# Two token tiles per state burst and two token chunks per denominator burst, in a gated mix of linear attention and dilated local attention

## Chip, cores and metric

The kernel runs on one core of a Trainium2 chip. The metric is device time in microseconds, the median of several executions. Nearly all differences in this study are below 0.3% (1.5 us of 488), so each run was timed in rounds with the kernel before on the same chip. A ratio is the mean time of one kernel's fast runs over the mean of the other's in the same rounds; it is not quite the ratio of the quoted medians.

## The reference

Two attention blocks read the same tokens (2048 tokens, width 1024, 32 heads of 32) and are mixed by a gate per token.

```python
g = sigmoid((x * gate_w).sum(-1))
a = A(x, A_wqkv, A_wo)      # linear attention
b = B(x, B_wqkv, B_wo)      # softmax over 8 keys, 2 tokens apart
return g * a + (1 - g) * b
# A: phi(t) = where(t > 0, t + 1, exp(t)) + 1e-6
#    kv  = sum over tokens of phi(k) outer v     (a 32x32 state per head)
#    z   = sum over tokens of phi(k)
#    o   = phi(q) @ kv / (phi(q) . z + 1e-6);  A = o @ wo
```

The *state* of A is `kv` with `z` as a 33rd column. The *denominator* is `phi(q) . z`.

## The kernel before

The program makes a list of operations, each with an engine, an assumed cost, operands and a priority. A list scheduler orders them per engine, and the order is then fixed: every engine executes its list, waiting on semaphores. PSUM banks are chosen while the list is made. The kernel plans six times and keeps the plan whose estimated length is least.

```python
class Pool:                                   # who gets which PSUM bank
    def next(self):
        if seen is None:                      # first plan: in turn
            b = self.bs[self.n % len(self.bs)]
        else:                                 # later plans: the bank that the plan before freed first
            b = min((b for b in self.bs if ...), key=lambda b: seen[b.take] ...)
        ...

for _ in range(PASSES):                       # PASSES = 6
    got = plan(seen)
    seen = got[2]
    if best is None or got[0].span < best[0].span:
        best = got
```

The stages on TensorE are: B's values; B's keys and queries; A's keys and values (16 token tiles of 128); A's query features (4 token chunks of 512, 8 groups each); A's outputs; B's final product. Between dense groups (8 matmuls of 128x128 by 128x512) there are bursts of small matmuls:

* *scores* and *values* of B's local attention, 18 times each;
* *state*, one burst per token tile, into a PSUM bank, which VectorE adds to a running sum:

```python
def state(t, pkt, azt):
    bank = main.next()
    def fn(e):
        for s in range(8):
            for c in range(4):
                h = 16 * (s // 4) + 4 * c + s % 4
                last = e.matmul(bank.ap()[32*c:32*c+32, s*33:s*33+33], pkt[:, h*32:(h+1)*32], azt[:, h, :],
                                start=True, stop=True, tile_position=(0, 32 * c))
        return last
    P.op("pe", fn, 0.22, mode="c", ...)
    # VectorE: copy (t == 0), otherwise kva += bank
...
states.append((slot_n[0] + 4, lambda ...: state(t, pkt, azt)))     # some groups after its tile
```

* *folds*: the state is multiplied into A's output weights (4 bursts); a fold needs four banks at once;
* *denominators*, one burst per chunk of 512 tokens. ScalarE makes reciprocals, DMAs write them to memory and read them back broadcast over 32 rows, and VectorE multiplies the query features by them:

```python
def over(u):                                   # chunk u
    db = main.next()
    # 8 matmuls of 128x32 by 128x512, four column tiles at a time
    P.op("pe", fn, 0.55, mode="c", ...)
    # ScalarE: Ln, Exp(-x);  4 writes to memory
    for j in range(8):                         # read back, multiply
        P.op("sp", ... dma_start(B, src), ..., lat=1.0)
        P.op("dve", ... tensor_tensor(dst, dst, B, ALU.mult), 0.65, ...)

for n, (u, j) in enumerate(nums):              # 32 query groups
    numer(u, j)
    if j == 7:
        after(3, lambda u=u: over(u))
    ...
    if n >= 20:
        a_out(*outs.pop(0))                    # an output may not start before its chunk is divided
EARLY = 3
for t in range(EARLY):                         # some of B's final tiles go between outputs
    while len(outs) > 8:
        a_out(*outs.pop(0))
    final(t)
while outs:
    a_out(*outs.pop(0))
```

## Time and profile before

| | before |
|---|---|
| time, median of the first 3 runs | 488.56 us |
| span of the profiled run | 486.2 us |
| TensorE busy | 474.9 us |
| VectorE busy | 288.4 us |
| dense matmuls, start to start | 215.8 ns |

The page of the kernel before: engines (busy us, share of the span, instructions), and the chain of work that ended last.

```profile
span 486.2 us, 10107 instructions
...
PE 474.9 (98%) x4336; PEld 222.2 (46%) x4403; DVE 288.4 (59%) x557; ACT 139.0 (29%) x225; POOL 5.5 (1%) x34
...
PE 95%; DVE 2%; issue 1%; DMA 1%; SPq 0%; ACT 0%; DVEq 0%
```

TensorE is the limit everywhere, so only what shortens TensorE's own list, or one of its few waits, counts.

What TensorE waited for in the kernel before (us in total, times, longest):

```profile
PE ps_all L1333 <- issue: 3.2, 20, 0.2
PE ps_all L1372 <- DVE warm L1282: 1.3, 1, 1.3
PE ps_all L1333 <- DMA xT<-in_A_x_dram: 0.8, 2, 0.6
PE ps_all L1333 <- DVE rs L1471: 0.5, 3, 0.2
PE ps_all L1333 <- ACT e L1340: 0.2, 1, 0.2
```

The timeline of TensorE in the kernel before (start us, duration us, line, instruction, out<-in, form, count, idle before): one state burst by itself, one behind a values burst, then the four denominator bursts.

```profile
201.85 0.38 PE L1547 MATMUL ps_all<-az,pk 128*32 128x33 bf16 x32
202.17 3.63 PE L1333 MATMUL ps_all<-w,xT 128*128 128x512 bf16 x15
205.73 0.68 PE L1462 MATMUL ps_all<-v,E 64*57 64x33 bf16 x64
206.34 0.38 PE L1547 MATMUL ps_all<-az,pk 128*32 128x33 bf16 x32
...
331.96 0.61 PE L1626 MATMUL ps_all<-pq,zsel 128*32 128x512 bf16 x8
...
348.15 0.62 PE L1626 MATMUL ps_all<-xT,zsel 128*32 128x512 bf16 x8
...
366.07 0.61 PE L1626 MATMUL ps_all<-xT,zsel 128*32 128x512 bf16 x8
...
394.35 0.62 PE L1626 MATMUL ps_all<-xT,zsel 128*32 128x512 bf16 x8
```

A duration in these rows is not what a burst costs, since neighbouring rows overlap (the dense row starts at 202.17 us, before the state row ends at 202.23). The cost is read from the dense matmuls on its two sides: from the start of the last dense one before it to the start of the first one after it, less the 215.8 ns that the first of them takes anyway. A state burst alone comes to 0.405 us, a denominator burst to 0.641 us.

### The profile page before, as it was taken

How to read it: one execution, taken by the hardware profiler on the slowest of the kernel's cores; microseconds unless marked ns; L12 is line 12 of the kernel's file. 1: busy time of each engine (PE TensorE's matmuls, PEld its weight loads, DVE VectorE, ACT ScalarE, POOL GpSimd, SP SyncE). 2: the span in 40 equal slices, each digit the busy share in tenths (PEclk: the TensorE clock that was granted, in tenths of full speed). 3: DMA queues.
4: the chain of work that ended last, by engine and by line, in shares of the span. 5: the costliest groups of instructions: out<-in, count | busy, mean ns of one | idle time of the engine just before them, and what ended most of it. 6: DMA issues, size and time to landing. Idle time of an engine off the chain costs nothing.

```text
span 486.2 us, 10107 instructions
## 1 busy us (share of the span) xinstructions
PE 474.9 (98%) x4336; PEld 222.2 (46%) x4403; DVE 288.4 (59%) x557; ACT 139.0 (29%) x225; POOL 5.5 (1%) x34
## 2 busy tenths in 40 slices
PE   8999999999999999999999999999999999999997
PEld 3444444444444444444444544444444444444443
DVE  2112336899788888575666656596865735434444
ACT  2111111214322233324534333455423322010000
POOL 4000000000000000000000000000000000000000
PEclk9999999999999999999999999999999999999999
DMA  8999992222014459423312322822674316101212
GB/s 221 225 208 309 357 361 63 85 89 87 2 43 142 106 153 233 99 77 84 77 44 65 98 55 48 200 51 41 160 190 98 99 17 179 43 24 44 88 67 89
DMA packets 72951, 57.39 MB, mean 118 GB/s; under 512 B 37953, under 2 KB 60865, under 8 KB 72898
## 3 DMA queue, kind: packets, MB, share of 16 engines
q1 hardware_dynamic: 72210, 56.07, 43.1%
q8 instruction: 36, 0.59, 0.5%
q10 hardware_dynamic: 688, 0.59, 0.4%
q14 instruction: 17, 0.14, 0.1%
HBM read 34.49 MB, written 13.76 MB: 99 GB/s over the span
## 4 chain that ended last, share of the span: by engine, by line
PE 95%; DVE 2%; issue 1%; DMA 1%; SPq 0%; ACT 0%; DVEq 0%
PE ps_all L1333 78%; PE ps_all L1675 11%; PE ps_all L1462 2%; PE ps_all L1439 2%; DMA xT<-in_A_x_dram 1%; PE ps_all L1547 1%; DVE zsel L1589 1%; PE ps_all L1626 0%; DVE pq L1346 0%; SPq L1307 0%; PE ps_all L1599 0%; SPq L1312 0%; DVE rs L1471 0%; DVE e L1344 0%; ACT e L1340 0%
## 5 line engine op out<-in xcount | busy, mean ns | idle before, releaser
L1333 PE MATMUL ps_all<-w,xT 128*128 128x512 bf16 x921 | 209.1, 379 | 4.6 <-issue 1.9
L1333 PE MATMUL ps_all<-xT,w 128*128 128x512 bf16 x747 | 168.3, 379 | 2.0 <-issue 1.3
L1333 PEld LDWEIGHTS ps_all<-w,xT 128*128 128x128 bf16 x960 | 91.1, 98 | 109.6 <-DMA xT<-in_A_x_dram 1.8
L1333 PEld LDWEIGHTS ps_all<-xT,w 128*128 128x128 bf16 x768 | 73.7, 98 | 89.0 <-issue 1.8
L1675 PE MATMUL ps_all<-w,qT 128*128 128x512 bf16 (+1 forms) x259 | 55.3, 372 | 0.3
L1675 PEld LDWEIGHTS ps_all<-w,qT 128*128 128x128 bf16 x264 | 25.8, 98 | 29.7
L1364 DVE CAST vst<-ps_all 128x512 bf16<-128x512 f32 x15 | 10.4, 694 | 43.1 <-PE ps_all L1333 43.1
L1447 ACT ACTIVATE E<-ps_all 128x1824 bf16<-128x1824 f32 (+1 forms) x18 | 30.4, 1687 | 13.4 <-PE ps_all L1439 13.4
L1344 DVE TENSOR_SCALAR e<-e 128x512 bf16<-128x512 bf16 x64 | 17.9, 283 | 26.6 <-ACT e L1342 15.6
L1679 DVE SCALAR_TENSOR_TENSOR o<-ps_all,gm,xT 128x512 bf16<-128x512 f32 (+1 forms) x25 | 18.1, 729 | 23.1 <-PE ps_all L1675 22.9
L1342 ACT ACTIVATE e<-ps_all 128x512 bf16<-128x512 f32 x32 | 19.1, 597 | 42.8 <-PE ps_all L1333 42.8
L1340 ACT ACTIVATE e<-ps_all 128x512 bf16<-128x512 f32 x32 | 19.1, 597 | 36.1 <-PE ps_all L1333 35.3
L1294 DVE TENSOR_TENSOR mx<-mx,kT 128x1024 bf16<-128x1024 bf16 x32 | 20.7, 686 | 9.3 <-ACT kT L1365 9.2
L1294 DVE TENSOR_TENSOR mx<-mx,qT 128x1024 bf16<-128x1024 bf16 x32 | 20.8, 686 | 6.6 <-ACT qT L1368 6.6
L1365 ACT ACTIVATE az<-ps_all 128x512 bf16<-128x512 f32 x22 | 13.2, 599 | 38.3 <-PE ps_all L1333 38.3
L1365 ACT ACTIVATE vst<-ps_all 128x512 bf16<-128x512 f32 x17 | 10.2, 599 | 47.5 <-PE ps_all L1333 47.5
L1473 DVE TENSOR_TENSOR ot<-ps_all,rs 128x512 bf16<-128x512 f32 x36 | 23.6, 683 | 0.2 <-DVE rs L1471 0.2
L1450 DVE TENSOR_TENSOR E<-E,msk 128x1824 bf16<-128x1824 bf16 (+1 forms) x18 | 19.9, 1103 | 5.8 <-ACT E L1447 5.2
L1346 DVE SCALAR_TENSOR_TENSOR pk<-ps_all,e 128x512 bf16<-128x512 f32 x32 | 21.9, 687 | 0.6
L1365 ACT ACTIVATE kT<-ps_all 128x512 bf16<-128x512 f32 x17 | 10.1, 597 | 39.8 <-PE ps_all L1333 39.8
L1368 ACT ACTIVATE qT<-ps_all 128x512 bf16<-128x512 f32 x17 | 10.1, 597 | 39.0 <-PE ps_all L1333 38.9
L1642 DVE TENSOR_TENSOR xT<-xT,rb 128x512 bf16<-128x512 bf16 x24 | 16.3, 688 | 8.5 <-DMA rb<-rc_hbm 8.4
(72 smaller groups left out, 259.1 us busy)
## 6 DMA issues: line engine op xcount, KB each, us to landing
rb<-rc_hbm SPq DMA_DIRECT2D x32, 256.0 KB, 5.0
w<-in_A_wqkv_dram SPq DMA_DIRECT2D x6, 1024.0 KB, 8.6
v<-vB_hbm SPq DMA_DIRECT2D x36, 132.0 KB, 3.0
vB_hbm<-vst SPq DMA_DIRECT2D x32, 132.0 KB, 6.2
w<-in_B_wqkv_dram SPq DMA_DIRECT2D x4, 1024.0 KB, 8.6
xn<-in_A_x_dram SPq DMA_DIRECT2D x16, 256.0 KB, 2.8
out_dram<-o SPq DMA_DIRECT2D x15, 256.0 KB, 2.1
oB_hbm<-ot SPq DMA_DIRECT2D x36, 96.0 KB, 2.1
```

Source lines behind the costliest of these rows:

```text
L1294: P.op("dve", lambda e, m=m, op=op: e.tensor_tensor(m[:, 0:n], m[:, 0:n], src, op), 0.08 + n / 1920.0, reads=[m.all(), reg], writes=[m.all()],
L1333: last = e.matmul(bank.ap(), lhs(dc), rhs(dc), start=(dc == 0), stop=(dc == 7))
L1340: P.op("act", lambda e: e.activation(e_[:, :], bank.ap(), ACT.Exp), act(512), reads=[bank.iv], writes=[e_.all()])
L1342: P.op("act", lambda e: e.activation(e_[:, :], bank.ap(), ACT.Exp, accum_out=qe[:, col:col + 1]), act(512) + 0.1, reads=[bank.iv], writes= ...
L1344: P.op("dve", lambda e: e.tensor_scalar(e_[:, :], e_[:, :], 1.0, 1e-6, op0=ALU.min, op1=ALU.add), 0.25, reads=[e_.all()], writes=[e_.all()])
L1346: P.op("dve", lambda e: e.scalar_tensor_tensor(out=dst, in0=bank.ap(), scalar=0.0, in1=e_[:, :], op0=ALU.max, op1=ALU.add), dps(512), read ...
L1365: fa = lambda e: e.activation(dst, src(), ACT.Copy)
L1447: P.op("act", lambda e: e.activation(E[:, 0:32 * nq].rearrange("p (j q) -> p j q", j=4), ps[:, 4:8, 0:8 * nq], ACT.Exp), act(32 * nq), rea ...
L1450: P.op("dve", lambda e: e.tensor_tensor(ev(), ev(), m[:, :, :].rearrange("p r q -> p (r q)")[:, None, :].to_broadcast([128, 16, 2 * nq]), ...
L1473: P.op("dve", lambda e, r=r, bv=bv, h=h: e.tensor_tensor(o[:, 512 * h:512 * h + 512].rearrange("p (k i c) -> p k i c", k=2, c=32), bv()[:, ...
L1675: last = e.matmul(bank.ap(0, f1 - f0), qT[:, dc, t * 128:(t + 1) * 128], ws[3][:, dc, f0:f1], start=(dc == 0), stop=(dc == 7))
L1679: P.op("dve", lambda e, bank=bank, o_=o_, t=t, n=n, i0=i0, i1=i1, tgt=tgt, c0=c0: e.scalar_tensor_tensor(out=o_[:, i0 * 128:i1 * 128].rear ...
```

## The change

State bursts take two token tiles, accumulate them in PSUM, and ride inside a values burst, so that TensorE's tiling mode changes less often; VectorE adds half as often. Denominator bursts take two chunks. Since the first chunk's reciprocals come later for that, the scheduler gets a later landing time for the broadcast reads, the multiplications get a lower priority, five instead of three of B's final tiles go between the outputs, and they go ahead of the last 16 outputs instead of the last 8. Buffers for two more token tiles are found by moving other buffers.

```diff
@@ landing model: how long after its queue turn a DMA is taken to have landed
-                fin = dma_free + 2.0
+                fin = dma_free + o.pad                  # 2.0 unless given
@@ buffers
-    vr = Ring([... "v%d" ... range(3)])
+    vr = Ring([... "v%d" ... range(2)])
-    pk = Ring([... range(2)]);  az = Ring([... range(2)])
+    pk = Ring([... range(4)]);  az = Ring([... range(4)])
@@ values burst
-                P.op("pe", each, 0.55, mode="c", ..., name="PV")
+                fns, rd, wr, add = [each], [vt.all(), E.all()], [s.iv for s in SO], None
+                if len(states) > 1 and states[1][0] <= slot_n[0]:
+                    fn, more, bank, add = state([states.pop(0)[1] for _ in range(2)])
+                    fns, rd, wr = fns + [fn], rd + more, wr + [bank.iv]
+                P.op("pe", lambda e: [f(e) for f in fns][-1], ...)
@@ a pair that found no values burst
+            if len(states) > 1 and states[1][0] + 2 <= slot_n[0] and not later:
+                ...                                     # a burst of its own
@@ state of two tiles
                 for s in range(8):
-                    for c in range(4):
-                        ... start=True, stop=True, tile_position=(0, 32 * c))
+                    for i, (t, pkt, azt) in enumerate(two):
+                        for c in range(4):
+                            ... start=(i == 0), stop=(i == len(two) - 1), tile_position=(0, 32 * c))
@@ denominators of two chunks
-        def over(u):
-            db = main.next()
+        def over(*us):
+            dbs = [main.next() for _ in us]
             ...                                         # one burst, then Ln, Exp, writes, reads per chunk
-                                  chan="rci%d" % bs, lat=1.0)
+                                  chan="rci%d" % bs, lat=0.6, pad=4.0)
-                P.op("dve", ... ALU.mult), 0.65, ...)
+                P.op("dve", ... ALU.mult), 0.65, ..., prio=1000 + len(P.ops) + (120 if u % 2 else 80))
-            if j == 7:
-                after(3, lambda u=u: over(u))
+            if j == 7 and u % 2:
+                after(3, lambda u=u: over(u - 1, u))
-        EARLY = 3
+        EARLY = 5
-            while len(outs) > 8:
+            while len(outs) > 16:
```

More of the change, by code (lines that the diff above doesn't have):

```diff
@@ L59 @@
 class Op:
-    __slots__ = ("eng", "fn", "cost", "deps", "prio", "seq", "chan", "lat", "pos", "val", "users", "raw", "name", "mode", "start", "end")
+    __slots__ = ("eng", "fn", "cost", "deps", "prio", "seq", "chan", "lat", "pos", "val", "users", "raw", "name", "mode", "pad", "start", "end")
 class Prog:
@@ L78, in __init__, with op @@
         self.read = set()
-    def op(self, eng, fn, cost, reads=(), writes=(), prio=None, chan=None, lat=0.0, after=(), name="", mode="m"):
+    def op(self, eng, fn, cost, reads=(), writes=(), prio=None, chan=None, lat=0.0, after=(), name="", mode="m", pad=2.0):
         o = Op()
+        o.pad = pad
         o.eng, o.fn, o.cost, o.prio, o.chan, o.lat, o.name, o.mode = eng, fn, cost, prio, chan, lat, name, mode
@@ L1186, in build_kernel @@
     eps = SB([128, 1], F32, "eps")
-    gwb = SB([128, 1024], BF16, "gwb")
     gt = SB([128, NT], F32, "gt")
@@ L1196, in build_kernel @@
     flag = SB([1, 1], I32, "flag")
-    warm = SB([128, 512], BF16, "warm")
     er = Ring([SB([128, 512], BF16, "e%d" % i) for i in range(3)])
@@ L1206, in build_kernel @@
     rs = Ring([SB([128, 16], F32, "rs%d" % i) for i in range(4)])
-    vr = Ring([SB([128, 33 * H], BF16, "v%d" % i) for i in range(3)])
-    mtmp = [SB([128, 2, 57], BF16, "mt%d" % i, at=vr.t[2].lo + 256 * i) for i in range(2)]
+    vr = Ring([SB([128, 33 * H], BF16, "v%d" % i) for i in range(2)])
+    mtmp = [SB([128, 2, 57], BF16, "mt%d" % i, at=ot.t[1].lo + 256 * i) for i in range(2)]
     base[0] = max(base[0], top_)
@@ L1212, in build_kernel @@
     RBr = Ring([SB([128, 512], F32, "rb%d" % i, at=kT.lo + 2048 * i) for i in range(12)])
-    mxr = SB([1, 4, 128], F32, "mxr", at=vr.t[2].lo)
+    mxr = SB([1, 4, 128], F32, "mxr", at=ot.t[1].lo)
     ph = base[0]
     mx = [SB([128, 1024], BF16, "mx%d" % i, at=ph + 2048 * i) for i in range(2)]
-    pk = Ring([SB([128, 1024], BF16, "pk%d" % i) for i in range(2)])
-    az = Ring([SB([128, H, 33], BF16, "az%d" % i) for i in range(2)])
+    pk = Ring([SB([128, 1024], BF16, "pk%d" % i) for i in range(4)])
+    az = Ring([SB([128, H, 33], BF16, "az%d" % i) for i in range(4)])
+    warm = SB([128, 512], BF16, "warm", at=pk.t[2].lo)
+    gwb = SB([128, 1024], BF16, "gwb", at=pk.t[3].lo)
     xn = Ring([SB([128, 1024], BF16, "xn%d" % i, at=az.t[i].lo) for i in range(2)])
@@ L1464, in each @@
                     return last
-                P.op("pe", each, 0.55, mode="c", reads=[vt.all(), E.all()], writes=[s.iv for s in SO], name="PV")
+                fns, rd, wr, add = [each], [vt.all(), E.all()], [s.iv for s in SO], None
+                if len(states) > 1 and states[1][0] <= slot_n[0]:
+                    fn, more, bank, add = state([states.pop(0)[1] for _ in range(2)])
+                    fns, rd, wr = fns + [fn], rd + more, wr + [bank.iv]
+                P.op("pe", lambda e: [f(e) for f in fns][-1], 0.55 + 0.5 * (len(fns) - 1), mode="c", reads=rd, writes=wr, name="PV" if add is None else "PV+kv")
+                if add is not None:
+                    add()
                 o, os_ = ot.next()
@@ L1496, in slot @@
                 later.pop(0)[1]()
-            while states and states[0][0] <= slot_n[0]:
-                states.pop(0)[1]()
+            if len(states) > 1 and states[1][0] + 2 <= slot_n[0] and not later:
+                fn, rd, bank, add = state([states.pop(0)[1] for _ in range(2)])
+                P.op("pe", fn, 0.42, mode="c", reads=rd, writes=[bank.iv], name="kv")
+                add()
             pace[0] = min(pace[0] + rate, 1.0) if todo else 0.0
@@ L1537, in plan, with state, add @@
             P.op("pool", lambda e, z=z: e.memset(z[:, :, 32:33], 1.0), 0.2, writes=[z.part((0, H), (32, 33))])
-        def state(t, pkt, azt):
+        def state(two):
             bank = main.next()
             def fn(e):
-                last = None
                 for s in range(8):
-                    for c in range(4):
-                        h = 16 * (s // 4) + 4 * c + s % 4
-                        last = e.matmul(bank.ap()[32 * c:32 * c + 32, s * 33:s * 33 + 33], pkt[:, h * 32:(h + 1) * 32], azt[:, h, :],
-                                        start=True, stop=True, tile_position=(0, 32 * c))
-                return last
-            P.op("pe", fn, 0.22, mode="c", reads=[pkt.all(), azt.all()], writes=[bank.iv], name="kv")
-            src = lambda: bank.ap(0, 264).rearrange("p (i c) -> p i c", c=33)
-            if t == 0:
-                P.op("dve", lambda e: e.tensor_copy(kva[:, :, :], src()), dps(264), reads=[bank.iv], writes=[kva.all()])
-            else:
-                P.op("dve", lambda e: e.tensor_tensor(kva[:, :, :], src(), kva[:, :, :], ALU.add), dps(264), reads=[bank.iv, kva.all()], writes=[kva.all()])
+                    for i, (t, pkt, azt) in enumerate(two):
+                        for c in range(4):
+                            h = 16 * (s // 4) + 4 * c + s % 4
+                            last = e.matmul(bank.ap()[32 * c:32 * c + 32, s * 33:s * 33 + 33], pkt[:, h * 32:(h + 1) * 32], azt[:, h, :],
+                                            start=(i == 0), stop=(i == len(two) - 1), tile_position=(0, 32 * c))
+                return last
+            def add():
+                src = lambda: bank.ap(0, 264).rearrange("p (i c) -> p i c", c=33)
+                if two[0][0] == 0:
+                    P.op("dve", lambda e: e.tensor_copy(kva[:, :, :], src()), dps(264), reads=[bank.iv], writes=[kva.all()])
+                else:
+                    P.op("dve", lambda e: e.tensor_tensor(kva[:, :, :], src(), kva[:, :, :], ALU.add), dps(264), reads=[bank.iv, kva.all()], writes=[kva.all()])
+            return fn, [x.all() for _, p, a in two for x in (p, a)], bank, add
         for t in range(NT):
@@ L1573, in plan @@
                 if r == 3:
-                    states.append((slot_n[0] + 4, lambda t=t, pkt=pkt, azt=azt: state(t, pkt, azt)))
+                    states.append((slot_n[0] + 1, (t, pkt, azt)))
                 slot(FILL)
@@ L1617, in plan, with fn, spread @@
         last_in = [None]
-        def over(u):
-            tgt, c0 = pqn(u)
-            db = main.next()
-            def fn(e):
-                for q in range(2):
-                    for c in range(4):
-                        last = e.matmul(db.ap()[32 * c:32 * c + 32, :], zsel[:, 2 * c + q, :], tgt[:, 2 * c + q, c0:c0 + 512], start=(q == 0), stop=(q == 1),
-                                        tile_position=(0, 32 * c), skip_group_check=True)
-                return last
-            P.op("pe", fn, 0.55, mode="c", reads=[zsel.all(), tgt.part((0, 8), (c0, c0 + 512))], writes=[db.iv], name="den")
+        def over(*us):
+            dbs = [main.next() for _ in us]
+            def fn(e):
+                for u, db in zip(us, dbs):
+                    tgt, c0 = pqn(u)
+                    for q in range(2):
+                        for c in range(4):
+                            last = e.matmul(db.ap()[32 * c:32 * c + 32, :], zsel[:, 2 * c + q, :], tgt[:, 2 * c + q, c0:c0 + 512], start=(q == 0), stop=(q == 1),
+                                            tile_position=(0, 32 * c), skip_group_check=True)
+                return last
+            P.op("pe", fn, 0.1 + 0.45 * len(us), mode="c", reads=[zsel.all()] + [t.part((0, 8), (c, c + 512)) for t, c in map(pqn, us)], writes=[db.iv for db in dbs], name="den")
+            for u, db in zip(us, dbs):
+                spread(u, db)
+        def spread(u, db):
+            tgt, c0 = pqn(u)
             R, rs = RAr.next()
@@ L1639, in over @@
                 last_in[0] = P.op("sp", lambda e, B=B, src=src: e.dma_start(B[:, :], src), 0.5, reads=[[("R", 4 * u + j // 2, 4 * u + j // 2 + 1, None)]], writes=[B.all()],
-                                  chan="rci%d" % bs, lat=1.0)
+                                  chan="rci%d" % bs, lat=0.6, pad=4.0)
                 dst, reg = tgt[:, j, c0:c0 + 512], tgt.part((j, j + 1), (c0, c0 + 512))
-                P.op("dve", lambda e, B=B, dst=dst: e.tensor_tensor(dst, dst, B[:, :], ALU.mult), 0.65, reads=[reg, B.all()], writes=[reg])
+                P.op("dve", lambda e, B=B, dst=dst: e.tensor_tensor(dst, dst, B[:, :], ALU.mult), 0.65, reads=[reg, B.all()], writes=[reg],
+                     prio=1000 + len(P.ops) + (120 if u % 2 else 80))
         def a_loc(t):
```

## The prediction

> **What bounds the kernel.** TensorE. The page gives PE 98% busy of a 486.2 us span, the chain of waits is 95% PE, and PE's wait list holds 6 us in all. In the timeline the dense 128x512 matmuls start 215.8 ns apart everywhere; 2048 of them (by the code) are 442 us. The other 44 us are the start (first dense work at 7 us), the tail, and bursts of small matmuls. From the starts of the dense matmuls around each burst, less 215.8 ns, a burst costs: scores 0.63 us (18 times), values 0.94 (18), state alone 0.405 (5 of 16), state beside values 0.307 more (11 of 16), denominators 0.64 (4). DVE (59%), ACT (29%) and DMA are no limits.
>
> **Taken off TensorE.** The matmuls stay; only drains go. The Trainium skill, "TensorEngine Tiling (Array Packing)", Key Properties, says a change of tiling mode drains the array. The trace agrees: state costs 0.405 us between dense groups and 0.307 where it shares the switch with values, so a saved switch is worth 0.10 us. By the code's slot arithmetic 7 of 8 pairs ride in a values burst and the last stands alone: 7 x 0.614 + 0.71 = 5.0 us against 5.4, a gain of 0.4. Denominators: 0.64 us is two rounds of 0.216 and 0.21 of drain; two bursts of four rounds save 2 x 0.21 = 0.4. Together 0.8 us, all on the critical path.
>
> **Elsewhere.** Eight of 16 state additions on DVE go (0.40 us each): not critical, worth nothing.
>
> **Given back.** The first chunk's denominators move from 332 us to about 345.5. From a denominator burst to the eighth multiplication took 17.2 to 18 us in all four (1.5 us of ACT, 3.2 of write issues, reads at about 1 us each). With the longer burst, and some of the second chunk's writes going first, chunk 0 is ready at about 363 to 366 us (estimate from these). The A outputs, which now start at 352, must wait for it; TensorE can run the query groups of chunks 2 and 3 meanwhile, but each waiting output already owns one of 8 PSUM banks, in program order. After nine query groups (about 362 us) the banks run out: a possible hole of 0 to 4 us at 360 to 368 us. A hole over 1 us has one chance in two. For chunks 2 and 3 the five early final tiles (17 us) and four outputs (7 us) cover the delay. The values' readout starts up to 0.6 us later, as the fused burst signals once; 3.4 us of dense work hides it.
>
> **Predicted time.** 488.3 us: 0.8 us of drains gone, part given back. Without a hole 487.7. Range 487.1 to 490.8. Faster by over 2%: 0.01; within 2%: 0.97; slower by over 2%: 0.02.
>
> **What would show it.** State bursts of 64 matmuls directly behind values (1.55 us extra together), two denominator bursts of 1.07 us, state additions x8, dense pace unchanged. The hole: PE idle before an output group, released by DVE's multiplication by the reciprocals, between 355 and 370 us; without it PE's waits stay near 6 us.
>
> **What would make it wrong.** Accumulating twice into the same 33 columns back to back could run slower than 9.6 ns a matmul; late reads could block DVE, in its fixed order, ahead of evacuations and hold TensorE for several us in the last stage; the new static order could disturb scores and values in the middle.

## The result

| | before | after |
|---|---|---|
| median, 6 runs each | 488.48 us | 487.43 us |
| lowest to highest | 488.10 to 489.16 | 487.20 to 487.88 |
| ratio, 95% interval | | 0.9979 (0.9967 to 0.9992) |
| span of the profiled run | 486.2 us | 486.0 us |
| TensorE busy / VectorE busy | 474.9 / 288.4 us | 474.7 / 285.2 us |
| state | 16 bursts, 5 of them alone | 8 bursts, 1 of them alone |
| denominators | 4 bursts of 0.641 us | 2 bursts of 1.073 us |

The change gains 1.05 us. The page of the changed kernel:

```profile
span 486.0 us, 10106 instructions
...
PE 474.7 (98%) x4339; PEld 223.0 (46%) x4403; DVE 285.2 (59%) x547; ACT 140.2 (29%) x227; POOL 5.9 (1%) x36
...
PE 95%; DVE 2%; issue 1%; DMA 1%; SPq 0%; ACT 0%
```

What TensorE waited for in the changed kernel:

```profile
PE ps_all L1334 <- issue: 3.5, 22, 0.2
PE ps_all L1373 <- DVE warm L1283: 1.3, 1, 1.3
PE ps_all L1334 <- DMA xT<-in_A_x_dram: 0.6, 2, 0.4
PE ps_all L1610 <- DVE pq L1347: 0.5, 1, 0.5
PE ps_all L1334 <- DMA w<-in_B_wqkv_dram: 0.2, 1, 0.2
PE ps_all L1334 <- ACT e L1341: 0.2, 1, 0.2
```

The fourth row is new: a weight fold (line 1610) waits 0.5 us for an evacuation of query features on VectorE. There is no wait for a multiplication by the reciprocals.

The timeline of TensorE in the changed kernel: a values burst with a state pair, the waiting fold, and the stage of the denominators.

```profile
197.12 0.68 PE L1463 MATMUL ps_all<-v,E 64*57 64x33 bf16 x64
197.74 0.66 PE L1556 MATMUL ps_all<-az,pk 128*32 128x33 bf16 x64
...
322.22 0.44 PE L1610 MATMUL ps_all<-w,kvT 32*32 32x512 bf16 x16 [0.50 <-DVE pq L1347]
...
346.08 0.61 PE L1638 MATMUL ps_all<-pq,zsel 128*32 128x512 bf16 x8
346.52 0.60 PE L1638 MATMUL ps_all<-xT,zsel 128*32 128x512 bf16 x8
347.06 22.62 PE L1334 MATMUL ps_all<-xT,w 128*128 128x512 bf16 x102
369.52 13.98 PE L1334 MATMUL ps_all<-w,pq 128*128 128x512 bf16 x62
...
393.79 1.05 PE L1638 MATMUL ps_all<-xT,zsel 128*32 128x512 bf16 x16
```

Behind the first denominator pair all 13 remaining query groups run without a gap, 347.1 to 369.5 us, and only then the outputs of chunk 0 (`w,pq`). The hole that I feared between 360 and 368 us did not open.

One caution about the two traces. The start-up, up to the arrival of the first tokens and weights, is luck: the first scores matmul started anywhere from 128.77 to 129.95 us in the 14 traces of this study. A spread of 1.2 us is more than the effect. So I compare traces by the time from the start of the first scores matmul to the end of the last matmul. It is 354.00 us before and 353.37 us after: 0.63 us less, where the medians say 1.05. The difference of 0.4 us was the first open question.

### The profile page after: what moved, and what is told of

The parts are those of the page before. It is cut to its first block, busy times and chain, and to the rows that moved or that the text cites. A ratio compares the mean times of both kernels' runs of the same rounds, so it can differ in the third digit from the quotient of the medians.

```text
span 486.0 us, 10106 instructions
## 1 busy us (share of the span) xinstructions
PE 474.7 (98%) x4339; PEld 223.0 (46%) x4403; DVE 285.2 (59%) x547; ACT 140.2 (29%) x227; POOL 5.9 (1%) x36
## 4 chain that ended last, share of the span: by engine, by line
PE 95%; DVE 2%; issue 1%; DMA 1%; SPq 0%; ACT 0%
PE ps_all L1334 78%; PE ps_all L1693 11%; PE ps_all L1463 2%; PE ps_all L1440 2%; DMA xT<-in_A_x_dram 1%; PE ps_all L1556 1%; DVE zsel L1600 1%; PE ps_all L1638 0%; DVE pq L1347 0%; SPq L1308 0%; DVE w L1365 0%; PE ps_all L1610 0%; SPq L1313 0%; ACT e L1341 0%; DVE e L1345 0%
## 5 line engine op out<-in xcount | busy, mean ns | idle before, releaser
L1334 PE MATMUL ps_all<-xT,w 128*128 128x512 bf16 x746 | 166.3, 379 | 2.1 <-issue 1.4
L1366 ACT ACTIVATE kT<-ps_all 128x512 bf16<-128x512 f32 x20 | 11.9, 596 | 38.2 <-PE ps_all L1334 38.2
L1369 ACT ACTIVATE qT<-ps_all 128x512 bf16<-128x512 f32 x19 | 11.3, 597 | 37.4 <-PE ps_all L1334 37.3
L1369 ACT ACTIVATE xT<-ps_all,g 128x512 bf16<-128x512 f32 x10 | 6.9, 687 | 45.1 <-PE ps_all L1334 45.1
```

The costliest lines, as they stand in the source:

```text
L1334: last = e.matmul(bank.ap(), lhs(dc), rhs(dc), start=(dc == 0), stop=(dc == 7))
L1366: fa = lambda e: e.activation(dst, src(), ACT.Copy)
L1369: fa = lambda e: e.activation(dst, src(), ACT.Copy, scale=scale)
```

## Experiments

Theory A said that saved drains are the whole gain and that one fold wait takes part of it back. The rivals: fewer additions on VectorE; the new order and priorities, not the pairing; or a wait in the kernel before that its first trace did not show. All results first; "inner" is the time from the first scores to the last matmul in the trace of that run, and each row's median of before is from the same rounds.

| run | what it is | median us | before us | ratio, 95% interval | inner us |
|---|---|---|---|---|---|
| before, first trace | | 488.48 | | | 354.00 |
| after, first trace | | 487.43 | 488.48 | 0.9979 (0.9967, 0.9992) | 353.37 |
| after_again | control | 487.28 | 488.37 | 0.9975 (0.9961, 0.9988) | 353.38 |
| den_only | denominator pairs alone | 487.48 | 488.37 | 0.9977 (0.9964, 0.9991) | 353.56 |
| kv_only | state pairs alone | 488.32 | 488.37 | 0.9992 (0.9978, 1.0006) | 354.60 |
| zsel_pool | after, 16 copies on GpSimd | 486.53 | 488.37 | 0.9964 (0.9950, 0.9978) | 352.82 |
| late_plan | after, later bank plan | 490.84 | 488.57 | 1.0043 (1.0026, 1.0060) | 356.69 |
| no_retune | after, scheduling as before | 504.61 | 488.57 | 1.0327 (1.0309, 1.0344) | 371.00 |
| state_alone | after, 16 state bursts, none by values | 488.23 | 488.57 | 0.9997 (0.9980, 1.0013) | 354.49 |
| two_adds | after, no accumulation in PSUM | 487.49 | 488.57 | 0.9981 (0.9964, 0.9998) | 353.41 |
| before_again | null control | 488.45 | 488.19 | 1.0007 (0.9993, 1.0021) | 354.43 |
| early_three | after, 3 early final tiles | 502.98 | 488.19 | 1.0311 (1.0295, 1.0326) | 368.23 |
| old_landing | after, old landing model and priorities | 488.85 | 488.19 | 1.0019 (1.0005, 1.0033) | 354.79 |
| landing_alone | before, new landing model and priorities | 487.80 | 488.31 | 0.9988 (0.9975, 1.0002) | 353.98 |

All were correct.

### after_again: the control

No edit. Expected:

> The changed kernel once more, as a control. The gain so far is 1.05 us between medians (ratio 0.9979, interval 0.9967 to 0.9992), while the two traces account for 0.4 us between the first scores and the end (state 0.37 less, denominators 0.42 less, a wait of one weight fold 0.44 more). Theory A (the drains are the whole gain, part of it lost to that fold wait): ratio near 0.9990 (0.4 to 0.8 us). Rival (something else in the new order gives the larger part): ratio stays at 0.998 and the trace shows more than 0.8 us gained at places other than the state and denominator bursts. Start-up can differ by 0.3 us from run to run (first dense matmul of tile 0 complete at 8.18 and 8.51 us in the two traces).

The gain is the same (0.9975) and the inner time repeats to 0.01 us. The rival's figure for the ratio came out, yet no part of the traces held more than the state and denominator bursts. So the missing 0.4 us had to be on the side of before.

### den_only and kv_only: each half alone

den_only is the kernel before with every part of the change that concerns denominators (landing model, priorities, five early tiles, pairs). kv_only is the changed kernel with these taken out:

```diff
-            if j == 7 and u % 2:
-                after(3, lambda u=u: over(u - 1, u))
+            if j == 7:
+                after(3, lambda u=u: over(u))            # and over(), priorities, EARLY as before
```

> The kernel before with the pairs of denominators, the landing model, the priorities and the five early final tiles, but the state as before (16 bursts, 11 beside a values burst). Theory A: two denominator bursts of 1.07 us in place of four of 0.64, 0.42 us less TensorE time, 488.0 us if before is 488.4; state bursts still 0.405 alone and 0.307 beside values. Rival (state side carries the gain): no measurable change.

> The changed kernel with the denominators, priorities and early tiles of before, so that only the state pairs are new. Theory A: state 5.08 us in all in place of 5.40 to 5.45, so 0.35 us less, and if the wait of the second weight fold appears (0.44 us in the changed kernel, behind the longer last state burst) the two cancel: 488.3 to 488.4. Rival (fewer additions on DVE help): over 0.6 us faster than before.

den_only has two bursts of 1.073 us, as expected, and its trace is 0.44 us shorter than the first trace of before. But its time gains 0.89 us between medians, twice what was expected. kv_only gains nothing clear. Its state is 0.6 us shorter, but the second fold waits 0.45 us longer, and two of its four denominator bursts took 1.03 and 1.04 us in place of 0.64: they waited. That was the hint: single denominator bursts can wait, and the first trace of before did not show it.

### before_again: a second trace of the kernel before

No edit. Expected:

> The kernel before, run as if it were a new one: a null control and a second trace. Measured from the first scores matmul (after the start-up, whose end varies by 1.2 us between traces) to the last matmul, the first trace of before took 354.00 us and the two of the changed kernel 353.37 and 353.38, a gain of 0.63 us, while times gain 1.05 to 1.1 us. If the missing 0.4 us is luck of that one execution of before: this trace has the same 354.0 us within 0.1, the ratio to before is 1.000, and the difference lies in the start-up or behind the last matmul. Rival (before has a wait in some executions that its first trace did not show): this trace shows over 354.2 us.

The rival is right. The inner time is 354.43 us, 0.43 us more than in the first trace, and the second and third denominator bursts cost 0.92 and 0.80 us in place of 0.64. The timeline of TensorE in this second trace of before:

```profile
348.38 0.61 PE L1626 MATMUL ps_all<-xT,zsel 128*32 128x512 bf16 x8 [0.21 <-DVE xT L1346]
```

The chain of waits of the same trace, around this burst (start us, us, what):

```profile
339.43 4.88 DMA rb<-rc_hbm
...
344.32 0.69 DVE pq L1642
345.01 0.60 DVE xT L1346
345.62 1.20 DVE pq L1642 x2
...
347.03 0.69 DVE pq L1642
347.72 0.61 DVE xT L1346
```

A broadcast read lands at 344.3 us. The multiplication that needs it (line 1642) stands in VectorE's fixed order ahead of the evacuations of query features (line 1346), so VectorE stops for the read; three more multiplications and two evacuations later the last feature of chunk 1 is ready, at 348.33 us, and only then can its denominators start. In the first trace the reads came a little earlier and TensorE never noticed.

### landing_alone: the order of VectorE without the pairing

The kernel before, with only two of the scheduler's changes:

```diff
-                                  chan="rci%d" % bs, lat=1.0)
+                                  chan="rci%d" % bs, lat=0.6, pad=4.0)
-                P.op("dve", ... ALU.mult), 0.65, ...)
+                P.op("dve", ... ALU.mult), 0.65, ..., prio=1000 + len(P.ops) + (120 if u % 2 else 80))
```

> The kernel before with only the landing model and the lower priority of the multiplications; denominators one chunk per burst, state as before. In the second trace of before the second and third denominator bursts took 0.80 and 0.92 us in place of 0.64, because the query features they read were evacuated on VectorE behind multiplications that waited for late reads (0.43 us in all). If the fixed order of VectorE is the cause, the multiplications that now come after the evacuations leave all four bursts at 0.64 us, first scores to last matmul takes 354.0 us, and the kernel is 0.2 to 0.5 us faster than before (ratio about 0.999). Rival (only having no single burst in the middle removes the waits): bursts of 0.8 to 1.0 us stay and the ratio is 1.000.

All four single bursts cost 0.641 us, the inner time is 353.98 us, and the median is 0.51 us below before. The interval (0.9975 to 1.0002) just includes no change, and bursts without a wait prove nothing by themselves, since the first trace of before had none either. What settles it is how early the features are ready. The last evacuation that the second denominator burst needs (the 16th), in the first trace of before and then in landing_alone, there with the burst:

```profile
347.38 0.68 DVE L1346 SCALAR_TENSOR_TENSOR xT<-ps_all,e 128x512 bf16<-128x512 f32 x1
...
344.67 0.68 DVE L1347 SCALAR_TENSOR_TENSOR xT<-ps_all,e 128x512 bf16<-128x512 f32 x1
...
347.93 0.62 PE L1627 MATMUL ps_all<-xT,zsel 128*32 128x512 bf16 x8
```

In the first trace of before it ended 0.1 us ahead of its burst, and the one for the third burst 0.2 us ahead of that: a read that lands half a microsecond later, as in the second trace, makes a wait. In landing_alone the two end 2.6 and 2.2 us ahead. So the fixed order of VectorE caused these waits, and the pairing is not needed to remove them. How much of the median comes from this stays open.

### state_alone: what a burst of its own costs

The changed kernel with one tile per state burst, never next to a values burst:

```diff
-                if len(states) > 1 and states[1][0] <= slot_n[0]:
-                    ...                                  # ride in the values burst
-            if len(states) > 1 and states[1][0] + 2 <= slot_n[0] and not later:
-                fn, rd, bank, add = state([states.pop(0)[1] for _ in range(2)])
+            if states and states[0][0] <= slot_n[0] and (slot_n[0] % 5 in (0, 1) or not todo and not later):
+                fn, rd, bank, add = state([states.pop(0)[1]])
```

> The changed kernel with the state one token tile at a time again, and none of its 16 bursts beside a values burst (14 between dense groups, 2 right behind scores). Same matmuls. Theory A (a burst pays a drain when it stands alone): 14 to 16 x 0.405 = 6.2 to 6.5 us of state against 5.08, so 1.1 to 1.4 us slower than the changed kernel, about 488.6 us. Rival (only the matmuls cost): 32 matmuls x 9.3 ns x 16 = 4.8 us, no slower.

14 bursts between dense groups cost 0.404 us each and 2 behind scores 0.31: 6.3 us, where the changed kernel pays 4.9. The inner time is 1.12 us longer; the fold wait, 0.45 us shorter here, hides the rest. The same matmuls cost more when TensorE leaves its dense matmuls for them more often. The Trainium skill says under "TensorEngine Tiling (Array Packing)", Key Properties, that a change of tiling mode drains the array; it gives no figure, and here one visit saved (out of the dense matmuls and back) is 0.10 us for state and 0.21 us for a denominator burst (1.073 is 2 x 0.641 less 0.21).

The visit is what has this price, not every change of tiling. Values (64 rows, tiles 64 columns apart) and state (128 rows, 32 columns apart) are different tilings too, so a state burst that rides still changes between them. But 32 more state matmuls cost 0.287 us both alone (0.691 less 0.404) and in a ride (0.595 less 0.308). That leaves 0.12 us for a visit of its own and only 0.02 us for the step from values to state (their difference is the 0.10). Why a visit costs 0.12 us for state and 0.21 for denominators, and that it is a drain, no run shows.

### two_adds: is it the additions, or the accumulation?

Pairs in one burst, but into two banks, with one addition each:

```diff
-            bank = main.next()
+            banks_ = [main.next() for _ in two]
-                                            start=(i == 0), stop=(i == len(two) - 1), tile_position=(0, 32 * c))
+                                            start=True, stop=True, tile_position=(0, 32 * c))
```

> The changed kernel with pairs in one burst, but each tile into a PSUM bank of its own and added by its own VectorE instruction: 16 additions as before, same bursts, no accumulation in PSUM. Theory A (VectorE's additions are off the critical path; the accumulation itself is free): same time as the changed kernel within 0.3 us apart from waits for the extra bank, burst of state beside values 0.59 us as there. Rival (half the additions is what pays, or accumulating slows the matmuls): slower by up to 3 us, or the burst faster than 0.59 us. The planner itself sees about 1.4 us of waiting for the extra bank here, so a wait in the middle stage may show.

487.49 us and an inner time of 353.41 us, against 353.37. In this trace and in that of early_three no dense record is missing, and both show a values burst with a pair at 1.302 us and one without at 0.707: the pair costs 0.595 us, whether it accumulates or not. So accumulating in PSUM costs nothing, and the eight additions that the change removes from VectorE are worth nothing in sum. The sum hides two differences, because the extra banks change the plan. The stage up to the first fold is 0.16 to 0.19 us longer (188.26 us, against 188.07 to 188.10 in the other kernels with pairs), 0.15 of it in one pause of the dense matmuls at 194.5 us. The four folds are 0.15 us shorter: the wait of the second fold is gone, and a query group ahead of it waits instead.

```profile
321.58 1.90 PE L1334 MATMUL ps_all<-xT,w 128*128 128x512 bf16 x8 [0.26 <-DVE w L1365]
```

Whether the pause at 194.5 us belongs to the additions or to the extra banks is not shown. What pays is that two tiles share one visit.

### zsel_pool: the fold that waits

The 16 tiny copies into the denominator selector move to GpSimd; TensorE's order stays the same, instruction for instruction.

```diff
-                P.op("dve", lambda e, ...: e.tensor_copy(zsel[32*r:32*r+32, c:8:4, k:k+1], kva[...]), 0.1, ...
+                P.op("pool", lambda e, ...: e.tensor_copy(zsel[32*r:32*r+32, c:8:4, k:k+1], kva[...]), 0.3, ...
```

> The changed kernel with its 16 tiny copies into the denominator selector moved from VectorE to GpSimd; the order on TensorE is instruction for instruction the same. They are 3.1 us of VectorE just ahead of the evacuations that the second weight fold waits for. If that fold waits because of them, its wait (0.50 us in the trace of the changed kernel) goes and the kernel is 0.4 to 0.5 us faster than after_again (ratio to it about 0.999). Rival (the fold waits for something else, such as its own operand): wait and time unchanged.

VectorE in the changed kernel, behind the last state addition:

```profile
315.07 0.35 DVE L1600 CAST zsel<-kva 32x2 bf16<-32x2 f32 x2
315.45 0.45 DVE L1596 STREAM_TRANSPOSE kvT<-kvb 128x256 bf16<-128x256 bf16 x1
315.93 2.72 DVE L1600 CAST zsel<-kva 32x2 bf16<-32x2 f32 x14
318.68 0.69 DVE L1347 SCALAR_TENSOR_TENSOR pq<-ps_all,e 128x512 bf16<-128x512 f32 x1
```

VectorE and the second fold in zsel_pool:

```profile
314.84 0.43 DVE L1596 STREAM_TRANSPOSE kvT<-kvb 128x256 bf16<-128x256 bf16 x1
...
316.33 0.69 DVE L1347 SCALAR_TENSOR_TENSOR pq<-ps_all,e 128x512 bf16<-128x512 f32 x1
...
320.81 0.43 PE L1610 MATMUL ps_all<-w,kvT 32*32 32x512 bf16 x16
```

With the two traces laid over each other at the first fold (317.73 and 316.89 us), the copies held back the two query evacuations ahead of the second fold by 2 to 3 us. Without them the wait is gone and the inner time falls by 0.56 us. But before has these copies too, and its second fold costs only 0.59 us. What the pairing changed can be read from the timelines, though no run isolates it: the copies end at 318.7 us in both, about 0.9 us after the first fold starts, but the order of VectorE then puts two evacuations of the first fold (0.69 us each) ahead of the query evacuation that the second fold waits for, where before put one. The median is 486.53 us, 0.75 us below after_again in the same rounds. This version beats both kernels.

### late_plan: where the feared hole is

The planner may not keep its first plan, so that banks go to the group that finds the earliest free one, which is the rule that the prediction reasoned from.

```diff
-        if best is None or got[0].span < best[0].span:
+        if _ > 0 and (best is None or got[0].span < best[0].span):
```

> The changed kernel, but its planner may not keep its first plan, in which PSUM banks go round in turn; it must take a later plan, in which each group takes the bank that the plan before frees first. My prediction's hole rested on that second rule (each waiting output owns a bank and the query groups run out of banks). Theory A (the hole was a property of that allocation, which the kernel does not use): query groups stall for want of a bank and outputs wait for the multiplications, PE idle 2 to 5 us between 355 and 375 us, about 490 to 492 us. Rival (the hole does not come because the reciprocals simply arrive in time): no wait, 487.4 us.

490.84 us. The timeline of TensorE in late_plan, behind the first denominator pair:

```profile
347.23 13.99 PE L1334 MATMUL ps_all<-xT,w 128*128 128x512 bf16 x64
362.89 1.90 PE L1334 MATMUL ps_all<-xT,w 128*128 128x512 bf16 x8 [1.67 <-DVE xT L1347]
366.23 12.26 PE L1334 MATMUL ps_all<-w,pq 128*128 128x512 bf16 x56 [1.44 <-DVE pq L1659]
```

After eight query groups the ninth waits 1.67 us for a bank, and the first output then waits 1.44 us for the last multiplication of chunk 0. This is the predicted hole, in place and in size (3.1 us, where 0 to 4 us was written). It belongs to a plan that the kernel did not keep. (The planner, run again for this check, estimates 485.8 us for its first plan and 489.4 us for each of the five later ones.) In the plan it kept, banks go round in turn, and since query groups and outputs alternate in the program they use alternate banks: waiting outputs hold four banks (7, 1, 3, 5 in the planner's list), and query groups keep the other four (0, 2, 4, 6).

### no_retune, early_three, old_landing: what the scheduler's part is for

Both parts of the scheduler's change undone, then each alone:

```diff
-        EARLY = 5                                 # early_three, no_retune
+        EARLY = 3
-            while len(outs) > 16:
+            while len(outs) > 8:
-     ... chan="rci%d" % bs, lat=0.6, pad=4.0)    # old_landing, no_retune
+     ... chan="rci%d" % bs, lat=1.0)
-     ... prio=1000 + len(P.ops) + (120 if u % 2 else 80))
+     ... )
```

> The changed kernel with the landing model, the priorities of the multiplications and the number of early final tiles (3) of before, so pairs alone. Theory A (pairs delay the reciprocals, and the retune only hides that): PE waits for multiplications by the reciprocals at the outputs of chunk 2, where 3 final tiles and 12 outputs... are replaced by the order of before: the third chunk is asked for about 20 us too early for its denominators, so a wait of 3 to 12 us, 491 to 499 us. Rival (the retune is decoration): 487.4 us, no wait over 1 us.

> The changed kernel with 3 early final tiles and 12 outputs ahead of them, as before; the landing model and priorities stay. The order on TensorE up to the second denominator burst is the same. Theory A (this one number carries the cover for the second pair): outputs of chunk 2 are asked for about 5.2 us after the burst while the eighth multiplication comes about 19 us after it, so one PE wait of 12 to 14 us released by that multiplication, about 504 us as in no_retune. Rival (landing model and priorities matter more): under 495 us.

> The changed kernel with the landing model and multiplication priorities of before and five early final tiles. The order on TensorE differs in the stage behind the first pair: outputs of chunk 0 are placed after 10 query groups instead of 13, at about 364 us. Theory A: the eighth multiplication ends at 364 to 367 us, so one PE wait of 0.5 to 2.5 us there, 488 to 490 us. Rival (no effect): 487.4 us.

The timeline of TensorE in early_three, behind the second denominator pair:

```profile
393.92 1.05 PE L1638 MATMUL ps_all<-xT,zsel 128*32 128x512 bf16 x16
394.90 5.35 PE L1334 MATMUL ps_all<-w,xT 128*128 128x512 bf16 x24
413.00 15.90 PE L1334 MATMUL ps_all<-w,xT 128*128 128x512 bf16 x64 [12.75 <-DVE xT L1659]
```

The outputs of chunk 2 are asked for 5 us after the end of their denominator burst and can start 18 us after it: a wait of 12.75 us, 15 us on the time. no_retune waits 13.05 us there. My upper bound of 499 us for no_retune was too low: the wait is longer than the 12 us that I allowed, 2.2 us more are lost between 360 and 366 us (old_landing loses 1.4 there), and I did not have the sequel of the wait, the clock. Granted clock in no_retune (us, PE, PEld, DVE, ACT and POOL busy with counts, PEclk, DMA share, GB/s):

```profile
401.50:415.00 13.50, 0.45 (x3) 0.02 (x2) 6.29 (x9) 0.69 (x1) 0.00 (x0) 0.66 0.87 225
415.00:421.50 6.50, 6.50 (x21) 2.52 (x22) 4.43 (x7) 0.69 (x2) 0.00 (x0) 0.66 0.88 249
```

Dense matmuls behind the pause start 427 ns apart for ten matmuls and then 216 again, 2 us lost. The Trainium skill, "TensorE: Matmul & The Clock Gate", Part 1, says an idle TensorE falls back to half its clock and needs a few microseconds of work to return; the trace agrees (the page gives 426.7 ns for 512 columns at half clock).

old_landing is mild. Its time is in the expected range, but not by the expected wait of an output for a multiplication: a query group waits 0.69 us for a bank, the second fold's 0.5 us stays, and the inner time is 1.42 us over that of the changed kernel; all of it lies between the two denominator bursts (49.12 us from start to start, against 47.71). So the placement of the early tiles is indispensable to pairs (15 us). early_three changes two numbers at once, how many tiles there are and how many outputs stay behind them, and no run separates these. The landing model and priorities are worth about 1.4 us with pairs (one trace), and 0 to 0.5 us without: landing_alone's inner time equals the first trace of before and is 0.45 us under the second.

## Why the prediction was right, and where it was not

The measured 487.43 us lies in the range, and below the 487.7 us written for a run without a hole. The range also holds 488.48 us, the time before, so lying in it shows little; the terms below are the test. That the gain of 1.05 us comes near the 0.8 us of saved visits is in part luck: two terms that I did not have, a loss of 0.45 us and a gain of up to 0.43 us, nearly cancel.

* **The limit.** Right. TensorE was and is 98% busy, and only its own list and its waits moved the time.
* **State.** Right in mechanism, a little small. 0.4 us was written; in complete records it is 5.41 us before (5 x 0.404 and 11 x 0.308) and 4.86 us after (7 x 0.595 and 0.69), 0.55 us. Seven pairs rode in values bursts and one stood alone, as derived from the code.
* **Denominators.** Right: 4 x 0.641 against 2 x 1.073 us, 0.42 us saved.
* **VectorE's additions.** Right: two_adds keeps all 16 and is as fast (within 0.2 us stage by stage).
* **The hole.** The step "each waiting output already owns one of 8 PSUM banks, in program order. After nine query groups (about 362 us) the banks run out" does not hold for the plan that the kernel keeps. late_plan shows that it holds for a later plan. I had reasoned from the second rule of the bank chooser without asking which of the six plans wins. The point forecast of 488.3 us contains 0.6 us for that hole, and this is the largest part of its error of 0.9 us. The arrival itself was sized well: the last multiplication of chunk 0 ended at 367.3 us, in a trace that started 0.5 us late, against 363 to 366 written (0.8 us beyond).
* **Missed, a loss.** The second fold waits longer: its burst costs 1.05 us in place of 0.59, so 0.45 us. zsel_pool shows that VectorE's queue ahead of it is the reason; why the pairing made it longer is read from the timelines alone. "PE's waits stay near 6 us" held as a sum only because most of that sum is missing records.
* **Missed, a gain.** Single denominator bursts in before wait for features that VectorE evacuates behind multiplications whose reads are late: 0.0 us in the first trace, 0.43 in the second, 0.78 in kv_only. The new order removes it (in the changed kernel the last evacuation ends 1.6 us ahead of each pair). This was invisible in the one trace that the prediction had.
* **A reading that was wrong.** "Values 0.94" is 0.71 us; one dense record was missing behind each values burst. The differences between bursts, on which the forecast rested, were not touched, since both sides had the same gap.

The sum, from traces: state -0.55 (by bursts) to -0.64 us (188.71 to 188.07 us from the first scores to the first fold), denominator drains -0.42, fold wait +0.45, denominator waits 0 to -0.43 in the two traces of before. Together that is -0.5 to -1.0 us, and -0.63 and -1.06 us as the inner times have it. What share of executions of before has how much of the last term stays open; two traces are not a distribution, but the medians (-1.05 and -1.09 us) are nearer to the second.

## What to carry to other kernels

When one engine is busy all the time, count how often it leaves its main work for small bursts and cost each visit from the starts of the neighbours; sharing a visit pays. Halving the work of an engine with time to spare does not, unless that work stands in its fixed order ahead of something that the busy engine waits for (the 16 copies of zsel_pool: 0.56 us). A change that delays a result must be paid for by other work that is placed under the delay: here the pairs cost 15 us with the early tiles placed as before. Below half a per cent take at least two traces of each side, anchor them behind the start-up, and check that the records are complete before a gap is called a cost.

## What the Trainium skill lacked or had wrong

* "TensorEngine Tiling (Array Packing)" says that a mode change drains the array but gives no cost. Here a visit saved, out of the dense matmuls and back, was worth 0.10 us (state burst of 128x32 tiles next to values) and 0.21 us (denominator burst), while the step from values to state, two different tilings, cost 0.02 us.
* "TensorE: Matmul & The Clock Gate", Back-to-back issue gap, gives about 131 ns per matmul as the sustained spacing for 512 columns in a stream of weight loads and matmuls. Here such a stream runs at 215.8 ns from end to end, which is the figure that the same page gives for the isolated gap.
* No page says that single matmul records can be missing in a regular place: in the first trace of before 67 of 2056 dense records were missing, and one of them lay behind each values burst, which made 0.71 us look like 0.94 and showed as 0.16 us of "issue".
* No page says how much the arrival of a kernel's first operands varies from run to run: the first scores matmul, behind it, came at 128.77 to 129.95 us in 14 traces.
